# A Fourier mixer and GeGLU kernel: a sixth sequence unit as seven block products, and five gate/up units in place of three made in the first quarter

## The chip, the cores and the metric

The kernel runs on one core of one Trainium2 chip. The metric is the device time of one execution in microseconds (us). Three timed runs of the kernel before gave 705.33, 707.02 and 707.19 us; their median is 707.02 us. "The trace" is one execution that was recorded by the hardware profiler.

## What is computed

The input x is 2048 x 448. Two sublayers follow each other, each behind a layer norm and with a residual:

```python
def _A_ref(x, dft_seq_re, dft_seq_im, dft_hid_re, dft_hid_im):
    a = jnp.einsum("bsd,ed->bse", x, dft_hid_re)
    b = jnp.einsum("bsd,ed->bse", x, dft_hid_im)
    y = jnp.einsum("ts,bse->bte", dft_seq_re, a) - jnp.einsum("ts,bse->bte", dft_seq_im, b)
    return y
def _B_ref(x, w_gate, w_up, w_down):
    g = jnp.einsum("bsd,df->bsf", x, w_gate)
    u = jnp.einsum("bsd,df->bsf", x, w_up)
    return jnp.einsum("bsf,fd->bsd", _gelu(g) * u, w_down)
h = x + _A_ref(_layernorm(x, axis=-1), ...)
h2 = h + _B_ref(_layernorm(h, axis=-1), ...)
```

The gate and up weights are 448 x 1792 each, the down weight is 1792 x 448. All inputs are 32-bit floats.

## The kernel before

**Numbers.** TensorE works on 16-bit halves. Each operand is split into a high part (ScalarE, `hi_part`, L106: a scaled copy to 16 bits) and a low part (VectorE, `lo_part`, L110 and L112: what the high part left over). A product then takes three matmuls: high by high, low by high, high by low.

**Stage one, the two transforms** (up to 348 us of the trace). Sixteen row tiles of x are normalised, split and turned (x_stats L354, x_lo, x_turn), and each gives two banks of features, a and b (`feature_mm`, L457, 22 matmuls of 448 columns). Two neighbouring tiles are a "unit" u of the sequence transform; there are 8 units and 8 passes p over the output rows. `seq_mm` (L574) multiplies the weights of one pass and unit (`wr`, 128 x 1024, loaded one by one) with the features of the unit's two tiles. A plain unit does it directly: 24 matmuls of 448 columns. A unit in `S_UNITS` does it as a 2 x 2 block product with seven products in place of eight: 42 matmuls of 224 columns. For that VectorE builds sums of weight blocks (`seq_sums`, L518 to L522) and splits them too (`wss`; L106 and L112), and once for each tile sums of features (`feature_sums`, L494 to L498, and `sums_low`, L110). Units 3 to 7 are done so, units 0 to 2 are plain. Of the raw weight blocks an S unit needs three; before, these lie in places 0, 2 and 3 of `wr`, so that each split is two instructions, of 256 and of 512 columns.

**Gate/up units.** The 14 column blocks f of gate and up are combined into seven-product form too (class `Weights`: sums L643 to L649, four splits). Eleven are made during stage one and stored to DRAM piece by piece (`w_dram`); they come back by a load of 896 KB (`gw_load`, L1073). Three, `LATE = {4: 0, 8: 7, 12: 15}`, are made in the first quarter of stage two: the number is the beat (half step) at which they begin. A late unit stays in its SBUF tile for the first quarter and is stored whole to DRAM (L698) for the other three.

**Stage two, the GeGLU** goes over four quarters q of the rows, with 14 steps each (t = 14 q + f). A step is a gate/up unit (class `GateUp`, 39 matmuls of 256 columns, L1199, in three PSUM banks X, Y, Z). From the second quarter on it holds a chunk of the down product of the quarter before as well (`dn_mm`, L1144, 21 matmuls of 224 columns). In a step VectorE reads Z and writes half of `hh` (L1209), reads Y and writes the other half (L1266), and reads Z again into `c12` (L1209, shown as `c`). TensorE closes Z (`z_close`) only after the first of these. `hh` of an odd quarter lives in the pool `odd_q`, which is opened on the place of the pool `scr` as the first quarter ends (`quarter0.close()`). `scr` holds, in the first quarter, raw gate/up weights and the weight tiles of units with f % 5 of 3 and 4.

**The down weight** comes in seven chunks n (`down_load`, L230, 448 KB each), of which GpSimd makes sums (`down_sums`, L235 to L238), ScalarE and VectorE splits (`down_hi`, `down_lo`). Before, chunks 0 and 1 are loaded ahead of the first quarter into two buffers, the tags `xn` and `tt` in turn, and the splits go on during steps 1 to 15.

**What sets the order.** Each engine and the load queue run their instructions strictly as written. In stage one a planner at build time (`arranged`) places tasks by costs and due times, which a table `SHIFT` moves by kind of task. In stage two the order is written by hand: the loop over t, `late_prep` for the late units, `down_prep` for the down weight, and the table `side` of extra work by step and place in the step. All DMAs are issued by SyncE (SP), also in order, so that one that waits holds all behind it. Their ends are counted on eight lanes (DMAHW0 to DMAHW7), given out in turn.

## Time and profile before

| | |
|---|---|
| timed runs, median of three | 707.02 us |
| the profiled execution, first to last instruction | 703.5 us |
| busy: TensorE, VectorE, ScalarE, GpSimd | 697.0, 563.2, 408.0, 198.8 us |
| granted TensorE clock | 0.999 |
| stage one / first quarter / the rest, about | 348 / 61 / 294 us |

The profile names for every recorded instruction its line in the kernel, its start and its length, what it waited for, and for a DMA the time from its issue to its landing. The 703.5 us are the time from the first to the last instruction of the profiled execution, and no other time of that execution is given; the timed runs are 3.5 us longer at the median. Steps are named by t, and "the first quarter" is t = 0 to 13.

### The profile page before, as it was taken

The page shows a single profiled execution, that of the slowest core. Times are in us where ns is not written, and L with a number is a line of the kernel's source. Part 1 is how long each engine was busy: PE and PEld are TensorE (multiplying, and loading weights), DVE is VectorE, ACT ScalarE, POOL GpSimd, SP SyncE. Part 2 cuts the span into 40 slices and gives each one's busy share as a digit, 9 for nine tenths or more (in the row PEclk, how much of TensorE's full clock was granted, in tenths as well). Part 3 has the DMA queues.
Part 4 walks back from the last instruction along what each step waited for, and adds up shares of the span by engine and source line. Part 5 has one row for each costly group of instructions (what it writes and reads, how often), then busy time and mean ns, then how long its engine had stood idle before and what let it go on. Part 6 is the DMA issues. An engine that isn't in the chain of part 4 may idle for free.

```text
span 703.5 us, 15378 instructions
## 1 busy us (share of the span) xinstructions
PE 697.0 (99%) x6046; PEld 584.1 (83%) x6046; DVE 563.2 (80%) x1170; ACT 408.0 (58%) x862; POOL 198.8 (28%) x225
## 2 busy tenths in 40 slices
PE   8999999999999999999999999999999999999998
PEld 5556578878787878778888889999999999999998
DVE  6999999999999897989578877575765755786786
ACT  5776674667576565656267765555555544455432
POOL 0000000000000000001136754474664745647342
PEclk9999999999999999999999999999999999999999
DMA  9554555687988867777579665658466594545401
GB/s 330 160 128 114 142 170 184 233 245 227 228 275 202 283 177 261 262 253 281 182 258 353 204 211 170 191 180 199 170 195 190 178 200 173 181 158 166 151 27 54
DMA packets 81849, 139.74 MB, mean 199 GB/s; under 512 B 41712, under 2 KB 59376, under 8 KB 81776
## 3 DMA queue, kind: packets, MB, share of 16 engines
q1 hardware_dynamic: 81776, 138.76, 63.5%
q8 instruction: 47, 0.77, 0.5%
q14 instruction: 26, 0.21, 0.1%
HBM read 109.25 MB, written 20.19 MB: 184 GB/s over the span
## 4 chain that ended last, share of the span: by engine, by line
PE 95%; DMA 1%; ACT 1%; DVE 1%; issue 1%; SPq 0%; ACTq 0%; DVEq 0%
PE acc L574 38%; PE acc_d L1144 15%; PE pY L1199 14%; PE pZ L1199 9%; PE pX L1199 9%; PE ab L457 9%; DMA x<-in_x_dram 1%; DVE dn_w L110 0%; ACT dn_w L106 0%; SPq L429 0%; ACT xn_h L254 0%; DVE st_x L354 0%; DVE hh L1209 0%; ACT wd L106 0%; ACT g L1252 0%
## 5 line engine op out<-in xcount | busy, mean ns | idle before, releaser
L1199 PEld LDWEIGHTS <-gw 128*128 128x128 f16 x2184 | 213.1, 98 | 23.7 <-issue 1.0
L574 PE MATMUL acc<-b,ws 128*128 128x224 f16 (+1 forms) x1296 | 204.6, 301 | 0.0
L574 PEld LDWEIGHTS <-ws 128*128 128x128 f16 x1296 | 125.6, 98 | 53.2
L1199 PE MATMUL pY<-hops,gw 128*128 128x256 f16 x952 | 129.1, 273 | 0.0
L1144 PE MATMUL acc_d<-wd,dn_w 128*128 128x224 f16 x1050 | 122.3, 259 | 0.0
L574 PE MATMUL acc<-b,wss 128*128 128x224 f16 x960 | 118.2, 259 | 0.0
L235 POOL TENSOR_TENSOR wd_s<-wd 128x448 f32<-128x448 f32 x7 | 10.1, 1442 | 346.8 <-DMA wr<-in_w_seq_dram 330.0
L1144 PEld LDWEIGHTS <-dn_w 128*128 128x128 f16 x1050 | 101.1, 98 | 2.9
L574 PEld LDWEIGHTS <-wss 128*128 128x128 f16 x960 | 92.3, 98 | 0.1
L106 ACT ACTIVATE ws<-wr 128x256 f16<-128x256 f32 (+2 forms) x104 | 62.4, 637 | 41.1 <-PE acc L574 16.1
L1199 PE MATMUL pZ<-hops,gw 128*128 128x256 f16 x616 | 85.5, 273 | 0.4 <-DVE hh L1209 0.3
L1276 POOL TENSOR_TENSOR hh<-hh,c 128x256 f32<-128x256 f32 x56 | 46.3, 828 | 139.7 <-ACT c L1274 139.5
L1199 PE MATMUL pX<-hops,gw 128*128 128x256 f16 x616 | 83.3, 273 | 0.0
L112 DVE SCALAR_TENSOR_TENSOR ws<-wr,ws 128x256 f16<-128x256 f32 (+2 forms) x104 | 70.6, 709 | 1.4 <-ACT ws L106 1.3
L110 DVE TENSOR_TENSOR dn_w<-hh,dn_w 128x256 f16<-128x256 f32 x50 | 25.3, 506 | 53.1 <-ACT dn_w L106 52.8
L106 ACT ACTIVATE wss<-wsum 128x1024 f16<-128x1024 f32 x40 | 42.1, 1053 | 36.8 <-DVE wsum L522 21.1
L457 PEld LDWEIGHTS <-xT 128*128 128x128 f16 x352 | 33.9, 98 | 32.8 <-ACT xT L420 1.5
L110 DVE TENSOR_TENSOR dn_w<-dn_s,dn_w 128x640 f16<-128x640 f32 x50 | 54.6, 1092 | 7.4 <-ACT dn_w L106 6.7
L1243 ACT ACTIVATE u<-pY 128x256 f32<-128x256 f32 x56 | 21.4, 382 | 61.4 <-PE pY L1199 61.3
L1291 POOL TENSOR_TENSOR dn_s<-hh 128x256 f32<-128x256 f32 x42 | 52.8, 1258 | 0.0
L112 DVE SCALAR_TENSOR_TENSOR wss<-wsum,wss 128x1024 f16<-128x1024 f32 x40 | 48.8, 1220 | 4.1 <-ACT wss L106 4.0
L1238 ACT ACTIVATE pY<-pX 128x256 f32<-128x256 f32 x56 | 20.6, 368 | 50.3 <-PE pX L1199 50.3
(120 smaller groups left out, 936.9 us busy)
## 6 DMA issues: line engine op xcount, KB each, us to landing
gw<-w_dram SPq DMA_DIRECT2D x53, 896.0 KB, 4.8
wr<-in_w_seq_dram SPq DMA_DIRECT2D x64, 512.0 KB, 4.4
gu_raw<-in_w_gu_dram SPq DMA_DIRECT2D x28, 384.0 KB, 4.8
w_dram<-gu_p SPq DMA_DIRECT2D x33, 256.0 KB, 3.1
hx<-in_x_dram SPq DMA_DIRECT2D x8, 448.0 KB, 4.5
h_dram<-hx SPq DMA_DIRECT2D x8, 448.0 KB, 4.8
hr<-h_dram SPq DMA_DIRECT2D x8, 448.0 KB, 5.3
x<-in_x_dram SPq DMA_DIRECT2D x7, 448.0 KB, 6.9
```

Source lines behind the costliest of these rows:

```text
L106: A.activation(dst, src, AF.Copy, scale=scale)
L110: V.tensor_sub(dst, src, hi)
L112: V.scalar_tensor_tensor(dst, src, scale, hi, op0=ALU.mult, op1=ALU.subtract)
L235: G.tensor_sub(s[:, 2:4], t[:, 0:2], t[:, 2:4])
L457: PE.matmul(feat[i][r][:, :D], xT[i][:, kx, :], w[:, kw, r * D : (r + 1) * D], start=n == 0, stop=n == 10,)
L574: PE.matmul(banks[k][:, cols], lhs, rhs, start=k not in begun, stop=stop, skip_group_check=True)
L1144: PE.matmul(acc[k // 2][:, k % 2 * HD : (k % 2 + 1) * HD], a_of(la, a), b_of(lb, b), start=first and m == 0 and k % 2 == 0, stop=last and ...
L1199: PE.matmul(ps, w[:, wl, wa + ws, :], ops[:, m + ms, :], start=first and n == 0, stop=last and n == len(terms) - 1, skip_group_check=True,)
L1238: A.activation(self.Y, self.X, AF.Copy)
L1243: A.activation(self.u2, self.Y, AF.Copy, scale=SC)
L1276: G.tensor_mul(c22, c22, self.c12)
L1291: E.tensor_sub(s[:, 2:4], t[:, 1:4:2], t[:, 0:4:2])
```

## The change

Unit 2 joins the S units, so that six of eight units are seven block products. The blocks of the sequence weights are renamed (`PRODUCTS`, `seq_sums`), so that the three raw blocks of an S unit lie side by side and one instruction of 768 columns splits them. The statistics of two of the eight pairs of x tiles (units 7 and 4) are taken by ScalarE, and parts of the reciprocal root move there (`half_of`, a Square). Gate/up units in the first quarter are now five, `LATE = {4: 0, 6: 5, 9: 10, 11: 15, 13: 19}`, each in five beats in place of six, so that nine are left to stage one. The split of the normalised h of pass 3 moves from stage one to steps 0 to 4 (`ffn_sums(1, 1, ...)` and what follows); that of quarter 2 begins at step 19 in place of 14. The down weight has one buffer, the tag `v` in stage two's pool, in place of two; its first chunk is loaded in step 4, its splits run from step 6 to step 19, and chunk n + 1 is loaded when the low part of chunk n is done. The planner has other costs and another `SHIFT`.

```diff
-    S_UNITS, WR_BUFS, WS_BUFS, WSS_BUFS, STAGE_BUFS = (3, 4, 5, 6, 7), 3, 3, 2, 2
+    S_UNITS, WR_BUFS, WS_BUFS, WSS_BUFS, STAGE_BUFS = (2, 3, 4, 5, 6, 7), 3, 3, 2, 2
+    BY_SCALAR = (7, 4)
...
+    def half_of(mv, tag, pool=small, of=1):
+        n = mv.shape[1]
+        r = pool.tile([P, 4, n], F32, tag=f"r{n}" if pool is small else f"r_{tag}", name=f"r_{tag}")
+        A.activation(r[:, 1], mv[:, :, 1], AF.Identity, scale=-0.5 / (of * X_SC**2), bias=half_eps)
+        return r
...
-        V.tensor_mul(r[:, 2], r[:, 0], r[:, 0])
+        if by_vector:
+            V.tensor_mul(r[:, 2], r[:, 0], r[:, 0])
+        else:
+            A.activation(r[:, 2], r[:, 0], AF.Square)
...
     def down_load(n):
-        wd32[n] = fops.tile([P, 4, HD], F32, tag="tt" if n % 2 else "xn", name=f"wd32_{n}")
+        wd32[n] = fpool.tile([P, 4, HD], F32, tag="v", name=f"wd32_{n}")
...
+    def x_moments(i, tiles):
+        if i == tiles[0]:
+            norm_x[tiles] = small.tile([P, 2, 2], F32, tag="mv2", name=f"mv_x{i}")
+        act_moments(norm_x[tiles][:, tiles.index(i), :], xt[i][0], junk)
...
-        V.tensor_add(s[:, 0:2], r[:, 1:2].to_broadcast([P, 2, 2 * P]), r[:, 0:4:3])
+        V.tensor_add(s[:, 0:2], r[:, 0:1].to_broadcast([P, 2, 2 * P]), r[:, 1:3])
...
-            return [(w[0], slice(0, 1), r[:, 0:1]), (w[0], slice(1, 3), r[:, 2:4])]
+            return [(w[0], slice(0, 3), r[:, 1:4])]
...
-    SHIFT = {"copy": -31.8, "fhigh": -68.2, "fhighp": -18.1, "flow": 9.9, "fsum": 12.9, "guhi": 1.2, "gulo":
+    SHIFT = {"copy": 481.5, "fhigh": -975.2, "fhighp": -890.3, "flow0": -229.1, "flow1": -167.7,
...
+    IN_FFN = 3
...
+            if p == IN_FFN:
+                continue
...
-    LATE = {4: 0, 8: 7, 12: 15}
+    LATE = {4: 0, 6: 5, 9: 10, 11: 15, 13: 19}
...
-    t = fixed(len(slots) - 14, 9, "SP", 0.1, lambda: down_load(0), last_e, lag=6.0, kind="dload")
-    fixed(len(slots) - 8, 9, "G", 4.0, lambda: down_sums(0), [t], kind="dsum")
...
-    down_load(1)
...
         n, odd = divmod(t, 2)
         if odd:
-            if n < NC:
+            if 0 <= n < NC:
                 down_lo(n, 1)
-                if n + 2 < NC:
-                    down_load(n + 2)
-            if n + 1 < NC:
+            if n + 1 < NC and n >= 0:
                 down_sums(n + 1)
-        elif n < NC:
+        elif 0 <= n < NC:
             down_hi(n, 0)
             down_lo(n, 0)
+            if n + 1 < NC:
+                down_load(n + 1)
+    WD0 = 6
+    def down_mid(t):
+        n, odd = divmod(t - WD0, 2)
+        if odd and 0 <= n < NC:
+            down_hi(n, 1)
...
+        (0, 1, lambda: ffn_sums(1, 1, (0,))),
...
+        (4, 4, lambda: down_load(0)),
+        (5, 4, lambda: down_sums(0)),
...
+        t0 = NF + 5 + 4 * j
+            (0 if j else -5, 1, lambda j=j: ffn_norm_act(2, j, hp[2, j])),
...
+    for f, n in LATE.items():
+        for k in range(5):
+            at(late_beats, n + k, (f, k))
...
-            if t > 0:
-                down_prep(t - 1)
+            do(t, 2)
+            down_prep(t - WD0)
             late_prep(2 * t + 1)
+            do(t, 4)
```

On SyncE, at the end of the first quarter, the DMAs stand as follows before (`gw` loads a unit's weights, `w_dram<-gw` stores a late unit, `wd32` loads a chunk of the down weight, `hr` loads rows of h; the brackets name the counters waited for):

```order
L1073 DMA gw13_5190<-w_dram13_164 128x3584 [waits DMAHW3_49,DMAHW1_49,PE_49]
L1073 DMA gw14_5253<-w_dram0_151 128x3584 [waits DMAHW6_49,DMAHW4_49,PE_49]
L230 DMA wd32_6_5317<-in_w_down_dram 128x896 [waits DMAHW5_49,DMAHW7_49,DVE_49,Pool_49]
L1073 DMA gw15_5384<-w_dram1_152 128x3584 [waits DMAHW0_49,PE_49]
L698 DMA w_dram12_163<-gw12_5149 128x3584 [waits DVE_49,Activation_49]
L1073 DMA gw16_5453<-w_dram2_153 128x3584 [waits DMAHW7_49,PE_49]
L1073 DMA gw17_5606<-w_dram3_154 128x3584 [waits DMAHW4_49,PE_49]
```

The same place on SyncE now (`gu_raw` loads the raw weights of a gate/up unit):

```order
L247 DMA wd32_2_5257<-in_w_down_dram 128x896 [waits DMAHW2_49,DMAHW4_49,DVE_49,Pool_49]
L673 DMA gu_raw13_5262<-in_w_gu_dram 128x768 [waits DMAHW7_49,DMAHW0_49,DVE_49]
L673 DMA gu_raw13_5262<-in_w_gu_dram 128x768 [waits DMAHW6_49]
L734 DMA w_dram9_162<-gw9_5051 128x3584
L1121 DMA gw14_5333<-w_dram0_153 128x3584 [waits PE_49]
L247 DMA wd32_3_5401<-in_w_down_dram 128x896 [waits DMAHW1_49,DMAHW4_49,DVE_49,Pool_49]
L734 DMA w_dram11_164<-gw11_5224 128x3584
L1121 DMA gw15_5475<-w_dram1_154 128x3584 [waits DMAHW3_49,DMAHW2_49,PE_49]
L247 DMA wd32_4_5539<-in_w_down_dram 128x896 [waits DMAHW1_49,DVE_49,Pool_49]
L1121 DMA gw16_5541<-w_dram2_155 128x3584 [waits DMAHW5_49,PE_49]
L734 DMA w_dram13_166<-gw13_5364 128x3584 [waits DMAHW6_49]
```

One store stood here and now there are three, for units 9, 11 and 13; the loads of the down weight, of which the last stood here, are now only at chunks 2 to 4, and the loads of units 14 to 16 stand between them.

On VectorE, as step 13 passes into step 14, the rows are before (`dn_w` is a split for the down product, `wd` one of the down weight; the last row is the first write into the second quarter's `hh`):

```order
L1209 SCALAR_TENSOR_TENSOR c12_12_5441<-pZ_12_5350,u2_12_5363 128x256 [waits PE_49,Pool_49]
L110 TENSOR_TENSOR dn_w0_5443<-hh0_4599,dn_w0_5443 128x256 [waits Activation_49]
L110 TENSOR_TENSOR dn_w0_5443<-dn_s0_5312,dn_w0_5443 128x640 [waits DVE_49,Activation_49]
L112 SCALAR_TENSOR_TENSOR wd_4572<-wd_s_5_5319,wd_4572 128x1120
L1209 SCALAR_TENSOR_TENSOR hh0_4599<-pZ_13_5415,u3_13_5479 128x256 [waits Activation_49]
L1266 SCALAR_TENSOR_TENSOR hh0_4599<-pY_13_5400,g1_13_5460 128x256 [waits PE_49]
L1209 SCALAR_TENSOR_TENSOR c12_13_5508<-pZ_13_5415,u2_13_5428 128x256 [waits PE_49,Pool_49]
L112 SCALAR_TENSOR_TENSOR wd_4572<-wd32_6_5317,wd_4572 128x448 [waits DMAHW5_49,Activation_49]
L110 TENSOR_TENSOR dn_w1_5527<-hh0_4599,dn_w1_5527 128x256 [waits Activation_49]
L110 TENSOR_TENSOR dn_w1_5527<-dn_s1_5378,dn_w1_5527 128x640 [waits DVE_49,Activation_49]
L1209 SCALAR_TENSOR_TENSOR hh1_5516<-pZ_14_5482,u3_14_5550 128x256 [waits DMAHW3_49,DMAHW1_49,Activation_49]
```

The same place on VectorE now:

```order
L1264 SCALAR_TENSOR_TENSOR c12_12_5530<-pZ_12_5437,u2_12_5450 128x256 [waits PE_49,Pool_49]
L112 TENSOR_TENSOR dn_w0_5532<-hh0_4652,dn_w0_5532 128x256 [waits Activation_49]
L112 TENSOR_TENSOR dn_w0_5532<-dn_s0_5395,dn_w0_5532 128x640 [waits DVE_49,Activation_49]
L114 SCALAR_TENSOR_TENSOR wd_4625<-wd32_3_5401,wd_4625 128x448 [waits DMAHW1_49,Activation_49]
L1264 SCALAR_TENSOR_TENSOR hh0_4652<-pZ_13_5504,u3_13_5567 128x256 [waits Activation_49]
L1321 SCALAR_TENSOR_TENSOR hh0_4652<-pY_13_5491,g1_13_5548 128x256 [waits PE_49]
L1264 SCALAR_TENSOR_TENSOR c12_13_5598<-pZ_13_5504,u2_13_5517 128x256 [waits PE_49,Pool_49]
L114 SCALAR_TENSOR_TENSOR wd_4625<-wd_s_3_5470,wd_4625 128x1120 [waits Activation_49]
L112 TENSOR_TENSOR dn_w1_5620<-hh0_4652,dn_w1_5620 128x256 [waits Activation_49]
L112 TENSOR_TENSOR dn_w1_5620<-dn_s1_5465,dn_w1_5620 128x640 [waits DVE_49,Activation_49]
L1264 SCALAR_TENSOR_TENSOR hh1_5609<-pZ_14_5572,u3_14_5643 128x256 [waits DMAHW6_49,DMAHW7_49,DVE_49,Activation_49]
```

The splits between are of chunk 3 in place of chunks 5 and 6, and the first write into `hh1` now waits on DMA lanes 6 and 7. Lane 6's last user ahead of it is the store of unit 13, whose tile (13 % 5 is 3) lies in `scr`; lane 7's is the store of unit 9.

More of the change, by code (lines that the diff above doesn't have):

```diff
@@ L92 @@
     G.memset(eps_t, EPS / X_SC**2)
+    half_eps = const.tile([P, 1], F32, name="half_eps")
+    G.memset(half_eps, -0.5 * EPS / X_SC**2)
     warm = const.tile([P, 1], F32, name="warm")
@@ L328 @@
     xt, xs, xT, norm_x = {}, {}, {}, {}
+    by_scalar = tuple((2 * u, 2 * u + 1) for u in BY_SCALAR)
+    junk = p1.tile([P, D], F16, name="junk")
     x_pairs = x.rearrange("(u g p) d -> u p g d", g=2, p=P)
@@ L501, in sums_high @@
     def sums_high(i):
-        t = bop[i] = dft.tile([P, 2, 7, HD], F16, name=f"b{i}")
+        if i == tiles_of[-1][1]:
+            t = p1.tile([P, 2, 7, HD], F16, tag="xs", name=f"b{i}")
+        else:
+            t = dft.tile([P, 2, 7, HD], F16, name=f"b{i}")
+        bop[i] = t
         hi_part(t[:, 0], b32[i][:, 1:8])
@@ L714 @@
     mixed = plain[:]
-    for n, s in zip((1, 3, 4, 5, 7), S_UNITS):
+    for n, s in zip((1, 2, 3, 5, 6, 7), S_UNITS):
         mixed.insert(n, s)
@@ L763, in chain @@
         for k, cost in enumerate(costs):
-            last = [add(engine, cost, due, lambda k=k: step(k == 0), after=last, kind=kind)]
+            on, cost = cost if isinstance(cost, tuple) else (engine, cost)
+            last = [add(on, cost, due, lambda k=k: step(k == 0), after=last, kind=kind)]
         return last[0]
@@ L834 @@
         room = [steps[where["U", *units[g - WS_BUFS]]]] if g >= WS_BUFS else []
-        size = 0.9 if is_s(u) else 1.0
-        high = add("A", size, T[n] - 1.6 if g else -20.0, lambda p=p, u=u: seq_high(p, u), begin=-4.0, after=[load] + room, kind="whigh" if g else None)
-        low = add("V", 1.02 if is_s(u) else 1.16, T[n] - 0.4 if g else -20.0, lambda p=p, u=u: seq_low(p, u), after=[high], kind="wlow" if g else None)
+        size = 0.82 if is_s(u) else 1.0
+        high = add("A", size, T[n] - 1.6 if g else -20.0, lambda p=p, u=u: seq_high(p, u), begin=-4.0, after=[load] + room, kind="whigh" if g else "whigh0")
+        low = add("V", 0.87 if is_s(u) else 1.16, T[n] - 0.4 if g else -20.0, lambda p=p, u=u: seq_low(p, u), after=[high], kind="wlow" if g else "wlow0")
         done_with[g] = [low]
@@ L867 @@
         m = [add("A", 1.75, t0 + 9.0 + 4 * g, lambda q=q, j=j, g=g, p=p: ffn_moments(q, j, hp[q, j], g, junk_of(e_of[p])), after=[mixed_in], kind="mom") for g in range(2)]
-        t = add("A", 0.25, t0 + 14.0, lambda q=q, j=j: ffn_root(q, j), after=m, kind="hroot")
-        t = chain("V", (0.2, 0.1, 0.1, 0.1), t0 + 15.0, lambda q=q, j=j: ffn_rstd_steps(q, j), [t], kind="hrstd")
+        t = add("A", 0.45, t0 + 14.0, lambda q=q, j=j: ffn_root(q, j), after=m, kind="hroot")
+        t = chain("V", RSTD, t0 + 15.0, lambda q=q, j=j: ffn_rstd_steps(q, j), [t], kind="hrstd")
         last_e, h_done[p] = m, [store, t]
@@ L1051 @@
             seq_mm(p, u, u == mine[0], u == mine[-1])
-        if t == p1_end:
-            first.close()
+    first.close()
     right.close()
@@ L1325, in dn_drain @@
     def dn_drain(p):
-        v = [ftile(f"v{k}", 1, f"v{k}_{p}", D) for k in range(2)]
+        v = fpool.tile([P, 2, D], F32, tag="v", name=f"v_{p}")
+        v = [v[:, k] for k in range(2)]
         return Drain(hr[p], acc_d[p], v, 1.0 / (H_SC * W_SC))
@@ L1416 @@
     odd_q = None
-    late_beats = {n + k: (f, k) for f, n in LATE.items() for k in range(6)}
-    assert len(late_beats) == 6 * len(LATE)
+    late_beats = {}
+    for f, n in LATE.items():
+        for k in range(5):
+            at(late_beats, n + k, (f, k))
     def late_prep(beat):
-        if beat not in late_beats:
-            return
-        f, k = late_beats[beat]
-        gu[f].beat(k)
-        after = [v for v in LATE if v > f]
-        if k == 3 and after:
-            gu_late(after[0])
-        if k == 5:
-            gw[f] = gu[f].w
+        for f, k in late_beats.pop(beat, ()):
+            gu[f].beat(k)
+            after = [v for v in LATE if v > f]
+            if k == 2 and after:
+                gu_late(after[0])
+            if k == 4:
+                gw[f] = gu[f].w
     cur = GateUp(0)
@@ L1451 @@
         d = t - NF
-        if d >= 0 and d % NC == 1:
+        if d >= 0 and d % NC == (4 if d // NC == 1 else 1):
             hr_load(d // NC)
@@ L1465 @@
                 gu[t].store()
-            if t > 0 and t % 2 == 0 and t < 2 * NC:
-                down_hi(t // 2 - 1, 1)
+            do(t, 1)
+            down_mid(t)
             nxt.z_open()
@@ L1556 @@
     part_store(7, 1, 1)
-    assert not side
+    assert not side and not late_beats
 def _tiles(inputs):
```

135 lines of the change are left out of this document (94 added, 41 removed).

## The prediction

> **What bounds the kernel now.** I read the page first, for the chain that ended last. Its summary by engine:
>
> ```profile
> PE 95%; DMA 1%; ACT 1%; DVE 1%; issue 1%; SPq 0%; ACTq 0%; DVEq 0%
> ```
>
> Nearly all of that chain is matmuls, so a change gains what it takes off TensorE (PE) and loses every stretch in which PE has to wait. Next I read the same chain in order of time (start, length, line, matmuls). `acc` rows are the sequence transform: x24 is one plain unit, x42 one unit of seven products. `pX` and `pY` rows are steps of the first quarter.
>
> ```profile
> 61.82 4.03 PE acc L574 x42
> 65.85 8.32 PE ab L457 x44
> 74.17 4.54 PE acc L574 x24
> ...
> 99.38 248.30 PE acc L574 x2100
> ...
> 400.92 1.20 PE pX L1199 x11
> 403.43 1.20 PE pY L1199 x11
> 405.18 1.20 PE pX L1199 x11
> ```
>
> The 2100 matmuls are 21 plain and 38 seven-product units: 21 x 4.54 + 38 x 4.03 = 248.5 us, against 248.30. From 99 to 348 us PE waits for nothing. Two `pX` rows are 405.18 - 400.92 = 4.26 us apart, which is a whole step: the first quarter is packed too. Last, the busy time of the engines by stage (columns: PE, PEld, VectorE = DVE, ScalarE = ACT, GpSimd = POOL):
>
> ```profile
> 27.80:99.40 71.60, 71.60 (x422) 40.95 (x421) 66.85 (x155) 49.48 (x80) 0.00 (x0) 1.00 0.55 144
> 99.40:347.70 248.30, 248.30 (x2102) 202.11 (x2101) 224.76 (x445) 153.52 (x291) 4.77 (x3) 1.00 0.76 237
> 347.70:409.30 61.60, 61.58 (x565) 54.95 (x564) 48.34 (x87) 42.62 (x100) 31.84 (x33) 1.00 0.74 258
> ```
>
> VectorE is the next in line: 291.6 of 319.9 us (91%) in stage one, 48.3 of 61.6 (78%) in the first quarter.
>
> **The sixth seven-product unit: PE gains.** In each of 8 passes 4.54 us become 4.03: 8 x 0.51 = 4.1 us off the path. All of it counts, since these rows have no wait between them. The price of 42 short matmuls depends on whether weight loads keep up:
>
> ```profile
> L574 PEld LDWEIGHTS <-ws 128*128 128x128 f16 x1296 | 125.6, 98 | 53.2
> ```
>
> A load is 98 ns here, and 42 pairs take 4.03 us, 96 ns a pair: loads just keep up. The Trainium skill (TensorE: Matmul & The Clock Gate, LDWEIGHTS (loading the stationary operand)) puts a load at its columns over 1.2, so 107 ns for 128; my estimate from that page is 42 x 107 = 4.48 us a unit and a gain of only 0.5 us. The measured row decides against it.
>
> **The same unit on VectorE.** The costliest rows by shape (count, busy, mean ns):
>
> ```profile
> L112 DVE SCALAR_TENSOR_TENSOR wss<-wsum,wss 128x1024 f16<-128x1024 f32 x40 | 48.8, 1220 | 4.1 <-ACT wss L106 4.0
> L112 DVE SCALAR_TENSOR_TENSOR ws<-wr,ws 128x1024 f16<-128x1024 f32 x24 | 29.7, 1238 | 1.0 <-ACT ws L106 0.9
> L518 DVE TENSOR_TENSOR wsum<-wr 128x512 f32<-128x512 f32 x40 | 28.4, 709 | 9.0 <-DMA wr<-in_w_seq_dram 8.8
> L112 DVE SCALAR_TENSOR_TENSOR ws<-wr,ws 128x512 f16<-128x512 f32 x40 | 27.3, 684 | 0.1
> ...
> L520 DVE TENSOR_TENSOR wsum<-wsum,wr 128x256 f32<-128x256 f32 x40 | 16.8, 419 | 0.3
> ```
>
> A pass gains sums (709 + 2 x 419) and their split (1220), and the raw split falls from 1238 to about 961 (768 columns, between the rows for 512 and 1024): 2.49 us, times 8 = 19.9. Raw blocks side by side save the other 40 units 684 + about 419 - 961 = 0.14 us each: 5.7. The unit's two feature tiles, by the rows of tile `b` (min/median/max ns):
>
> ```profile
> L112 DVE SCALAR_TENSOR_TENSOR b<-ab,b x12: 592/614/618, 21.9 to 55.2; 128x448 f16<-128x448 f32 x12
> L494 DVE TENSOR_TENSOR b<-b x10: 615/624/626, 38.2 to 100.2; 128x448 f32<-128x448 f32 x10
> L496 DVE TENSOR_TENSOR b<-b x10: 380/384/393, 39.4 to 100.9; 128x224 f32<-128x224 f32 x10
> L498 DVE TENSOR_TENSOR b<-b x10: 381/384/391, 40.7 to 101.3; 128x224 f32<-128x224 f32 x10
> L110 DVE TENSOR_TENSOR b<-b,b x10: 1782/1786/1793, 42.9 to 103.9; 128x1568 f16<-128x1568 f32 x10
> ```
>
> Each pays 624 + 2 x 384 + 1786 - 2 x 614 = 1.95 us: 3.9 for two. Against this two gate/up units leave, and the split of pass 3. First the busy time in stage one on `gu_s` (four sums and two of four splits, 11 units), then on `tt` (four row pairs):
>
> ```profile
> 27.00:348.00 321.00, 36.44 (x66) 13.48 (x22) 1.00 0.71 215
> ```
>
> ```profile
> 60.00:348.00 288.00, 12.23 (x36) 4.32 (x8) 1.00 0.72 223
> ```
>
> A unit is 36.44 / 11 + 0.684 + 0.419 = 4.4 us, two 8.8; the pass at least 12.23 / 4 = 3.1. Sum: 19.9 - 5.7 + 3.9 - 8.8 - 3.1 = +6.2 us, and x statistics and root steps that go to ScalarE take more off, which I leave unpriced. VectorE then has at most 297.8 of 315.8 us, 94%. It fits, with 18 us spare where there were 28. The cost lies between nothing and the whole 4.1 (if VectorE paced the stage); I take 0.5, near the lower end, since the 248.30 row shows no wait at 91%. ScalarE, at 203.0 of 319.9, has room for what it gets.
>
> **The first late unit.** Its raw weights are now loaded behind four stores of unit 12, whose last splits stand behind the last sequence split. Here are the loads (KB each, median us to landing), and that of the down weight:
>
> ```profile
> gw<-w_dram SPq DMA_DIRECT2D x53, 896.0 KB, 4.8
> wr<-in_w_seq_dram SPq DMA_DIRECT2D x64, 512.0 KB, 4.4
> gu_raw<-in_w_gu_dram SPq DMA_DIRECT2D x28, 384.0 KB, 4.8
> ...
> wd<-in_w_down_dram SPq DMA_DIRECT2D x7, 448.0 KB, 5.9
> ```
>
> If nothing hides it VectorE waits 4.8 us in step 0 ahead of what PE needs; if the stores are early it waits for nothing. I take 0.5.
>
> **The first quarter on VectorE.** It gets two late units (8.8) and the split of pass 3 (3.1 or more), and three of seven chunks of the down weight leave. At some 57 of 61.6 us (93%) it still fits, but runs late by up to a us, and its order is fixed.
>
> **The end of the first quarter: where I expect the loss.** The store of unit 13 must land before VectorE may write into the second quarter's `hh`, because the unit's tile lies where `hh1` goes. Stores of a late unit, us from issue to landing (min/median/max of three):
>
> ```profile
> DMA to landing us min/median/max: 8.0/8.6/9.2
> ```
>
> One of them in the load queue's timeline, and the `gw` load that waited for it, 8.67 us later:
>
> ```profile
> 401.36 0.38 SPq L698 DMA_DIRECT2D w_dram<-gw  x1
> 410.03 4.43 SPq L1073 DMA_DIRECT2D gw<-w_dram  x2
> ```
>
> The write into `hh1` and the matmuls that wait for it (they add to Z, which it reads), before:
>
> ```profile
> 412.84 0.41 DVE L1209 SCALAR_TENSOR_TENSOR hh<-pZ,u 128x256 f32<-128x256 f32 x1
> ```
>
> ```profile
> 413.40 0.71 PE L1199 MATMUL pZ<-hops,gw 128*128 128x256 f16 x5
> ```
>
> The earliest case: ahead of that store stand the loads of chunk 4 and unit 16. The first waits for the low part of chunk 3, which now stands where VectorE had this row:
>
> ```profile
> 406.69 1.32 DVE L112 SCALAR_TENSOR_TENSOR wd<-wd_s,wd 128x1120 f16<-128x1120 f32 x1
> ```
>
> It ends at about 407.3 (0.61 for 448 columns, as in tile `b`); with three issues of 0.3 the store goes at 408.2 and lands at 416.2 at the earliest. PE then goes on at 416.6 in place of 413.4: 3.2 us lost.
>
> The later case is a chain. With one buffer, chunk n + 1 is loaded only when GpSimd has summed chunk n. The sums of six chunks on GpSimd (third column; 18.96 / 6 = 3.2 us each):
>
> ```profile
> 348.30:411.00 62.70, 7.89 (x6) 6.77 (x6) 18.96 (x18) 1.00 0.73 254
> ```
>
> A round is 5.9 + 3.2 = 9.1 us, where two steps are 8.5. Chunk 0 is asked for behind the transposes that follow step 4, at about 372.5: step 5 starts at 405.18 - 8 x 4.26 = 371.1. It lands at 378.4, and after two more rounds and the sums of chunk 2, 399.8, the load of chunk 3 may go; VectorE's part of chunk 2, late in a full quarter, makes it 400.5. Behind it stands the store of unit 11 (landed 409.4), behind that, waiting for it, the load of unit 15, then chunk 4, unit 16 and the store of unit 13, at 410.4, landed 419.0. PE goes on at 419.4: 6.0 us lost. Nothing hides this, since PE is packed up to there and cannot pass `z_close`. Unit 15 itself lands at about 414.5, inside the same wait. The raw weights of unit 13, queued behind chunk 2 until 390.7, land at about 396, a us or two late in step 10; that wait is part of the 6.0, since the chain does not run by PE. I take 6.0, the later case, since every one of its links is written in the order; with loads at 7.0 and stores at 9.2 it would be 9.
>
> **The sum.** 703.5 - 4.1 + 0.5 + 0.5 + 6.0 = 706.4 us of span. The timed median is 3.5 above the span (707.02 against 703.5), so 709.9 us. A measurement of this kernel can tell about 0.3%, 2.1 us, from no change.
>
> **Rivals.** (1) The store is in time, and the change is faster. Price: 6.0 less, 703.9 us. It decides at a landing by 412.9, which needs a store of under 4.7 us at the earliest case. Against it speak all three stores (8.0 at least); for it, that a load of the same 896 KB takes 4.8 and that those stores ran beside other traffic. Chance 0.12. The Trainium skill (DMA: Bandwidth & Descriptors, Anatomy of one DMA) fits 2.0 us plus bytes over 436 GB/s for its path, an estimate of 4.1 us for this store, and warns that completion can be surprisingly late where HBM is written; by the formula the store would be in time, and the three measured stores contradict it. (2) The short chain: chunks land early, and only the earliest case holds. 3.2 in place of 6.0: 707.1 us, no change that can be told. Chance 0.22. (3) VectorE, at 94% in stage one, paces PE there as well: some 3 us more, 712.9. For it speaks that its order is strict; against it, that the unpriced x statistics leave it. Chance 0.10. (4) Weight loads set the pace and the PE gain is 0.5: 713.5. The 4.03 us row says no; 0.01. The forecast keeps 0.55, its own range 708.5 to 713.
>
> Faster takes rival 1 and a little: 0.13. Same takes rival 2 and the low edge of the forecast: 0.27. Slower is 0.60. The range, 704.2 to 714, leaves out half of rival 1 and the high end of the chain.
>
> **What would show it.** The plain units of pass 1 on: x42 in six of eight, and stage one ending some 4 us sooner. A wait of VectorE for a `w_dram` store at the first write into `hh`, with PE idle or stretched by 3 to 9 us around step 14. GpSimd waiting for `wd` loads in each odd step. I am wrong if the store of unit 13 lands before step 14 reaches `z_close`, or if stage one ends less than 3 us sooner.

## The result, and the profile after

The changed kernel takes 731.62 us (median of four runs, 730.01 to 734.46) against 706.35 us for the kernel before beside it: a ratio of 1.0366, with a 95% interval of 1.0339 to 1.0393. It is 25 us slower; the forecast was 3 us slower, with a range that ended at 714. The traced execution took 734.46 us, with a span of 732.7, so 1.8 us lie outside the span. (The forecast's 3.5 us were these 1.8 and the fact that the traced execution of before was, by these 1.8 us, the fastest of its three.) Of the executions reported below, two were disturbed, one of k1a and the traced one of k2b; they took some 1883 us and are left out of the medians.

The chain that ended last, by engine, was nearly all PE before. Now a quarter of it is something else:

```profile
PE 74%; DVE 10%; DMA 9%; ACT 3%; issue 2%; SPq 1%; POOL 1%; DVEq 0%; ACTq 0%
```

Where that quarter lies is shown by the busy time of the engines by stage, in the columns that the prediction showed. The stretches are stage one, the first quarter with the two steps behind it, the rest of the second quarter, and what is left:

```profile
27.50:343.70 316.20, 315.96 (x2663) 256.25 (x2662) 297.02 (x537) 212.35 (x365) 0.00 (x0) 1.00 0.64 196
343.70:440.00 96.30, 75.53 (x631) 64.23 (x629) 59.00 (x119) 49.10 (x118) 32.80 (x35) 0.90 0.68 220
440.00:520.00 80.00, 76.70 (x717) 69.86 (x716) 55.66 (x109) 43.79 (x104) 46.33 (x50) 0.99 0.58 182
520.00:732.70 212.70, 209.43 (x2024) 195.88 (x2022) 146.47 (x310) 100.45 (x253) 115.66 (x132) 1.00 0.49 156
```

Stage one is as forecast: PE waits 0.24 us in it, VectorE has 297.0 of 316.2 us (94%). All the loss is behind it. From 343.7 to 440 PE is idle for 20.8 us, and the granted clock (the column after POOL) is 0.90 where it was 1.00.

PE's timeline gives the stops, each with what ended it in brackets (start, length, matmuls):

```profile
342.33 0.64 PE L610 MATMUL acc<-b,ws 128*128 128x224 f16 x5
...
344.24 0.82 PE L1254 MATMUL pX<-hops,gw 128*128 128x256 f16 x6
...
354.00 0.81 PE L1254 MATMUL pZ<-hops,gw 128*128 128x256 f16 x6 [1.33 <-DVE c L1264]
...
371.68 1.36 PE L1254 MATMUL pY<-hops,gw 128*128 128x256 f16 x11
...
383.30 2.51 PE L1254 MATMUL pY<-hops,gw 128*128 128x256 f16 x11 [7.20 <-ACT pY L1293]
...
409.13 1.23 PE L1254 MATMUL pZ<-hops,gw 128*128 128x256 f16 x5 [4.37 <-DVE hh L1264]
...
436.28 1.22 PE L1254 MATMUL pZ<-hops,gw 128*128 128x256 f16 x5 [6.57 <-DVE hh L1264]
```

There are four stops over 1 us up to step 14, of 1.3, 7.2, 4.4 and 6.6 us; the shorter ones bring the sum to 24.0 us. Behind a long stop the same eleven matmuls take 2.51 us where they took 1.36 ahead of it. The engine named in the brackets was itself held by a DMA each time. For the stop of 1.3 us VectorE had waited 2.44 us for the raw weights of unit 4. For the three long ones it was first ScalarE, whose in-order queue stands at the high part of unit 9; then VectorE at the raw weights of unit 13, and at its first write into `hh1`:

```profile
381.77 0.94 ACT L108 ACTIVATE gw<-gu_raw 128x512 f16<-128x512 f32 x2 [8.85 <-DMA w_dram<-gw]
```

```profile
407.09 0.79 DVE L679 TENSOR_TENSOR gu_s<-gu_raw 128x384 f32<-128x384 f32 x1 [3.67 <-DMA gu_raw<-in_w_gu_dram]
...
435.80 0.42 DVE L1264 SCALAR_TENSOR_TENSOR hh<-pZ,u 128x256 f32<-128x256 f32 x1 [7.18 <-DMA w_dram<-gw]
```

Only the last of these is the wait that the prediction built on. The first is one that it did not see: units 4 and 9 both have f % 5 = 4, so unit 9 is made in the tile of unit 4, and its first write waits until unit 4 has been stored. That store stands in the load queue (start, time of issue) between two pairs of transposes, which are new there, since the split of pass 3 was moved into the first quarter:

```profile
369.07 3.72 SPq L332 DMA_TRANSPOSE hops<-xs  x2
372.89 0.54 SPq L1121 DMA_DIRECT2D gw<-w_dram  x1
373.47 0.43 SPq L734 DMA_DIRECT2D w_dram<-gw  x1
373.94 4.94 SPq L332 DMA_TRANSPOSE hops<-xs  x2
378.93 0.58 SPq L247 DMA_DIRECT2D wd<-in_w_down_dram  x1
```

The store was issued at 373.47 and landed at 381.75, though unit 4's last split had ended at 360.

PE's 24 us of stops do not make up the whole. PE is busy for 701.4 us where 697.0 - 4.1 = 692.9 were due, 8.5 us more. By the starts of the matmuls behind the three long stops, 6.8 of these are matmuls at a lower clock (1.8, 2.5 and 2.6 us). The rest is something else: k1b, below, is busy for 694.9 us at a clock of 1.00, also 2 us above what was due, and where those come from stays open. Together: 703.5 - 4.1 + 24 + 8.5 = 731.9, against a span of 732.7.

### The profile page after: what moved, and what is told of

It reads as the page before. It is cut to its first block, busy times and chain, and to the rows that moved or that the text cites. A ratio compares the mean times of both kernels' runs of the same rounds, so it can differ in the third digit from the quotient of the medians.

```text
span 732.7 us, 15592 instructions
## 1 busy us (share of the span) xinstructions
PE 701.4 (96%) x6190; PEld 600.4 (82%) x6190; DVE 579.7 (79%) x1140; ACT 422.8 (58%) x870; POOL 196.4 (27%) x226
## 4 chain that ended last, share of the span: by engine, by line
PE 74%; DVE 10%; DMA 9%; ACT 3%; issue 2%; SPq 1%; POOL 1%; DVEq 0%; ACTq 0%
PE acc L610 25%; PE acc_d L1191 14%; PE pY L1254 12%; PE pZ L1254 8%; PE pX L1254 8%; PE ab L489 7%; DMA wr<-in_w_seq_dram 3%; DMA w_dram<-gw 3%; DMA gu_raw<-in_w_gu_dram 2%; DVE ws L114 1%; DVE dn_w L112 1%; DVE wsum L554 1%; DVE wss L114 1%; DVE wd L114 1%; DMA w_dram<-gu_p 1%
## 5 line engine op out<-in xcount | busy, mean ns | idle before, releaser
L1254 PEld LDWEIGHTS <-gw 128*128 128x128 f16 x2184 | 216.3, 99 | 50.7 <-issue 24.9
L610 PE MATMUL acc<-b,ws 128*128 128x224 f16 (+1 forms) x1248 | 187.2, 288 | 0.2 <-DVE ws L114 0.2
L610 PEld LDWEIGHTS <-ws 128*128 128x128 f16 x1248 | 120.7, 98 | 36.1 <-DVE ws L114 0.7
L610 PE MATMUL acc<-b,wss 128*128 128x224 f16 x1152 | 141.7, 259 | 0.0
L610 PEld LDWEIGHTS <-wss 128*128 128x128 f16 x1152 | 110.8, 98 | 0.0
L108 ACT ACTIVATE wss<-wsum 128x1024 f16<-128x1024 f32 x48 | 50.6, 1054 | 47.3 <-DVE wsum L558 34.0
L108 ACT ACTIVATE ws<-wr 128x768 f16<-128x768 f32 (+1 forms) x64 | 56.8, 890 | 29.0 <-PE acc L610 16.6
L114 DVE SCALAR_TENSOR_TENSOR ws<-wr,ws 128x768 f16<-128x768 f32 (+1 forms) x64 | 65.0, 1018 | 0.5 <-ACT ws L108 0.5
L114 DVE SCALAR_TENSOR_TENSOR wss<-wsum,wss 128x1024 f16<-128x1024 f32 x48 | 58.6, 1220 | 3.1 <-ACT wss L108 2.7
L1293 ACT ACTIVATE pY<-pX 128x256 f32<-128x256 f32 x56 | 20.7, 369 | 48.4 <-PE pX L1254 48.3
L489 PE MATMUL ab<-wh_hi,xT 128*128 128x448 f16 x224 | 45.6, 352 | 1.2 <-DVE b L114 0.4
```

The lines of the kernel that those rows point to most:

```text
L108: A.activation(dst, src, AF.Copy, scale=scale)
L114: V.scalar_tensor_tensor(dst, src, scale, hi, op0=ALU.mult, op1=ALU.subtract)
L489: PE.matmul(feat[i][r][:, :D], xT[i][:, kx, :], w[:, kw, r * D : (r + 1) * D], start=n == 0, stop=n == 10,)
L610: PE.matmul(banks[k][:, cols], lhs, rhs, start=k not in begun, stop=stop, skip_group_check=True)
L1254: PE.matmul(ps, w[:, wl, wa + ws, :], ops[:, m + ms, :], start=first and n == 0, stop=last and n == len(terms) - 1, skip_group_check=True,)
L1293: A.activation(self.Y, self.X, AF.Copy)
```

## The experiments

**The single stops.** Each of four runs takes one cause away from the changed kernel. The first moves the store of unit 4:

```diff
             if k == 4:
                 gw[f] = gu[f].w
+                if f in (4,):
+                    gu[f].store()
...
-            if t in LATE:
+            if t in LATE and t not in (4,):
                 gu[t].store()
```

> The changed kernel, with the store of unit 4 issued right after its last split (step 2) in place of step 4. In its trace PE stops 7.2 us in step 6 while ScalarE waits for that store (issued 373.5, landed 381.8), and runs at half speed for some 4 us behind it (about 2.0 us more). Theory A, single waits: each stop of PE has one transfer as its cause, and its price is the stop and the slow stretch behind it, so the time falls by 9.2 to about 722.4. Theory B, the next in line: the load of chunk 0 of the down weight landed at 384.8, 3 us after the store, and ScalarE needs it one step later; then most of the stop stays under another name, and the time falls by 0 to 3, to 728.5 to 731.6.

Measured: 729.31 us, ratio to before 1.0326 (1.0302 to 1.0350), 2.3 us less than the changed kernel. The wait for the store is gone, and ScalarE stands a few microseconds later at the next late transfer, chunk 0 of the down weight:

```profile
381.42 0.58 ACT L108 ACTIVATE wd<-wd 128x448 f16<-128x448 f32 x1 [4.34 <-DMA wd<-in_w_down_dram]
```

PE stops for 0.7, 2.0 and 0.8 us there, 3.5 in place of 7.2, and no slow matmuls follow. By the median theory B holds: the store alone was not the price. The traced execution, at 726.80 us, was the fastest of the four, so B is right in kind, but half of the stop stays and not most of it. The next kernel loads chunk 0 ahead of the transposes as well:

```diff
-        (4, 4, lambda: down_load(0)),
+        (1, 1, lambda: down_load(0)),
```

> As e1, and the load of chunk 0 of the down weight is issued in step 1, ahead of the transposes, in place of behind them in step 4. Theory A: the same as e1, 722.4, since the load was not the cause. Theory B: only now does the stop of step 6 go, about 722.4 here and 728.5 or more in e1. Theory C, VectorE is the limit of the first quarter (it has no idle time from 387.3 to 403.4 in the changed kernel): the stop goes here, but the one near step 10 grows by some 4 us, and the time is about 726.

Measured: 725.59 us, 1.0284 (1.0267 to 1.0301), 6.0 less than the changed kernel. The stop of 7.2 us is gone but for 1.2 us. The time is the one that theory C gave, but not for its reason: the stop of step 10 became 3.9 us, no longer than before. What is left of the 9.2 us of theory A are small stops (1.9, 0.6, 1.2 and 1.1 us).

The third kernel stores unit 13, and only it, right after its last split (the edit of e1 with 13 for 4).

> The changed kernel, with the store of unit 13 issued right after its last split (step 11) in place of step 13, ahead of the loads of chunk 4 and units 15 and 16. The split ended at 419.2, the stop of 6.6 us began at 429.7, and stores took 8 to 10 us. Theory A: the store lands at 427.7 to 429.5, the stop goes with its slow stretch (2.7), and the time falls by 8 to 9.3, to about 723. Theory B: PE stops there for something else that comes as late (the load of unit 15, the splits of chunk 3), and the time falls by under 3.

Measured: 724.12 us, 1.0257 (1.0234 to 1.0280), 7.5 less. PE no longer stops for over 0.5 us around step 14. Theory A holds, though its 8 to 9.3 us were a little too much; the wait on which the forecast rested is real and is worth what it said, and a little more. The fourth gives the raw weights of unit 13 a buffer of their own:

```diff
-            self.raw = pool.tile([P, 2, 6, P], F32, tag="raw", name=f"gu_raw{f}")
+            self.raw = pool.tile([P, 2, 6, P], F32, tag="raw2" if f == 13 else "raw", name=f"gu_raw{f}")
...
-            if k == 2 and after:
+            if k == (0 if f == 11 else 2) and after:
                 gu_late(after[0])
```

> The changed kernel, with a buffer of its own for the raw weights of unit 13, which are loaded in step 7 in place of step 8 and need not wait until VectorE has split those of unit 11. Theory A: the stop of 4.4 us near step 10 and its slow stretch (2.7) go, 724.6; the stop at step 14 stays as it is, 6 to 7 us, since its store waits behind work of step 13 that moves along with PE. Theory D, the chain of the down weight's chunks does not run by PE (the later case of the forecast): what is gained at step 10 is lost at step 14, whose stop grows to 11 to 13 us, and the time stays within 2 us of 731.6.

Measured: 728.15 us, 1.0316 (1.0301 to 1.0332), 3.5 less, half of what theory A gave. The stop of 4.4 us became two of 1.7 and 1.3. At step 14, which PE now reached 4 us sooner, the stop is as long as ever:

```profile
432.09 1.23 PE L1254 MATMUL pZ<-hops,gw 128*128 128x256 f16 x5 [6.24 <-DVE hh L1264]
```

It was 6.6 us in e1 and 6.5 in e2 too. Theory D, which is the chain of the forecast, would have made it longer each time. It falls: the store of unit 13 waits behind the load of chunk 4, which waits for VectorE's low part of chunk 3 in step 13, and that moves along with PE.

**All of them.** The three edits together, with all late units stored right after their last split:

> The edits of e2, e3 and e4 together: every late unit is stored right after its last split, chunk 0 of the down weight is loaded in step 1, and the raw weights of unit 13 have a buffer of their own. They gave 6.0, 7.5 and 3.5 us apart. Theory A, single waits: they add up, 731.6 - 17.0 = 714.6, with no stop of PE over 2 us and its clock near 1.00 throughout. Theory C, VectorE (or the chain of chunks) is the limit of the first quarter: taking one stop away moves PE on to the next, and the three together give under 12 us, 719.6 or more.

Measured: 717.89 us, 1.0164 (1.0121 to 1.0207), 13.7 less of 17.0. The largest stop is 2.9 us and the clock is back at 1.00, but the fourteen stops of stage two still add up to 13.8 us, and the kernel is 11.6 us above before. The interval, 714.8 to 720.9 us, reaches from theory A's time to theory C's and does not decide; the trace does, since small stops have come where the long ones went, as theory C says.

**What a stop costs.** In the kernel before, copies that nothing reads hold ScalarE in step 6:

```diff
+    block = const.tile([P, 512], F32, name="block")
+    G.memset(block, 0.0)
...
+            for _ in range(15 if t == 6 else 0):
+                A.activation(block, block, AF.Copy)
             late_prep(2 * t)
```

> The kernel before, with fifteen copies of 512 columns on ScalarE (some 0.6 us each, 9 us in all) put ahead of its work in step 6, which nothing reads. ScalarE has some 1.5 us to spare in a step, so PE should stop once, for 7 to 8 us. Face value: the time rises by the stop alone, 7 to 8 us. The stretch theory: the granted clock falls behind a stop of this length, matmuls take twice their time for some 4 us, and the time rises by 2 to 2.7 us more than the stop, some 10 us.

Measured: 716.25 us, 1.0142 (1.0123 to 1.0161), so 10.0 us more (8.7 to 11.4) for one stop of 8.0 us: the stretch theory. The same edit with 7 in place of 15:

> As c15_stop_long, with seven copies in place of fifteen, some 3.9 us on ScalarE. Fifteen stopped PE for 8.0 us and cost 9.9. PE should stop for some 3.5 us here. Face value: 709.8. The stretch theory: stops of up to 2.0 us had no slow matmuls behind them in the traces so far, those of 3.9 and more had 1 to 2.7 us; a stop of 3.5 us costs another 1 to 2 us, 711 to 712.

Measured: 710.09 us, 1.0057 (1.0037 to 1.0076), so 4.3 us more (2.6 to 5.4) for a stop of 2.7 us: face value, by the time and by the clock behind it. The windows ahead of, in and behind the stop show the difference; first fifteen copies, then seven (the clock is the column after POOL):

```profile
370.00:381.00 11.00, 11.00 (x103) 9.85 (x101) 10.15 (x18) 9.31 (x20) 6.64 (x6) 1.00 0.85 306
381.00:389.70 8.70, 0.70 (x7) 0.48 (x6) 0.36 (x1) 8.35 (x15) 0.00 (x0) 0.76 0.91 359
389.70:397.00 7.30, 7.30 (x56) 6.04 (x56) 4.07 (x9) 3.96 (x12) 4.26 (x5) 0.82 0.11 24
397.00:405.00 8.00, 8.00 (x75) 7.17 (x74) 7.44 (x12) 6.41 (x16) 4.75 (x5) 1.00 0.44 156
```

```profile
370.00:382.00 12.00, 12.00 (x113) 10.73 (x111) 11.19 (x20) 10.29 (x23) 7.58 (x7) 1.00 0.80 292
382.00:386.00 4.00, 1.29 (x13) 1.01 (x11) 0.91 (x2) 3.90 (x9) 0.00 (x0) 1.00 1.04 413
386.00:393.00 7.00, 7.00 (x67) 6.29 (x65) 5.53 (x11) 4.96 (x12) 4.72 (x5) 1.00 0.92 316
```

Behind the stop of 8.0 us PE gets through 56 matmuls in 7.3 us, where full speed gives 67 in 7.0, the number behind the stop of 2.7 us. So the long stop pays again, some 1.3 us here by the starts of its matmuls, and the short one does not. A stop of 0.7 and 0.9 us in stage one that came with the edit in both runs makes up part of the rest; its cause stays open.

**Fewer late units.** f4 is the changed kernel with stores right after the last split, chunk 0 in step 1, and four late units; f3 has the three of before:

```diff
-    LATE = {4: 0, 6: 5, 9: 10, 11: 15, 13: 19}
+    LATE = {4: 0, 6: 5, 9: 10, 11: 15}
```

> The changed kernel with every late unit stored right after its last split and chunk 0 loaded in step 1, and with four late units in place of five: unit 13 is made in stage one again. With it go its store, its raw load and 4.4 us of VectorE from the first quarter, and VectorE in stage one rises from 297 to some 301 of 316 us (95%). Theory A: the stops at steps 10 and 14 go, and the one of step 6; left are some 1.5 us at step 0 and 3 us of small stops from step 15 on, so 706.4 - 3.7 + 5 = about 708. Theory E, VectorE is the limit of stage one too: stage one, 316.4 us in the changed kernel, grows by 2 us or more, and the time is 710 or more.

Measured: 721.34 us, 1.0216 (1.0195 to 1.0237).

> As f4, with the three late units of the kernel before (4, 8 and 12, in five beats each, at its own beats), so that eleven units are made in stage one beside the sixth seven-product unit. VectorE in stage one has some 306 of 316 us (97%). Theory A: no stop of the first quarter over 2 us is left, about 707. Theory E: stage one grows by 4 us or more against the changed kernel's 316.4, which takes the whole gain of the sixth unit, and the time is 710 or more.

Measured: 727.88 us, 1.0310 (1.0289 to 1.0331). Both times are in the range of theory E, but neither theory had the place right. The waits of PE, f4 first and then f3 (total, times, longest):

```profile
PE acc L610 <- ACT acc L595: 5.8, 1, 5.8
PE pY L1254 <- ACT u L1298: 3.1, 1, 3.1
```

```profile
PE pY L1254 <- ACT pY L1293: 9.7, 2, 9.1
PE pZ L1254 <- DVE c L1264: 5.0, 1, 5.0
```

In f4 the order of stage one no longer fits its work: a copy on ScalarE comes 5.8 us late at 245 us. In f3 PE keeps its pace through stage one, but its last two gate/up units are finished only behind it, and PE stands for 9.1 and then, at the raw weights of unit 4, for 5.0 us. The order had been set for nine units. So h1 and h3 repeat four and three late units with the planner's `SHIFT` set anew for each, unit 4's raw weights loaded ahead of units 2 and 3, and the chunks one step earlier:

```diff
-    gw_load(2)
-    gw_load(3)
+    gu_late(min(LATE))
+    gw_load(2)
+    gw_load(3)
...
-    gu_late(min(LATE))
...
-    WD0 = 6
+    WD0 = 5
...
-        s = wd_s[n] = fops.tile([P, 5, HD], F32, tag="xs", name=f"wd_s_{n}")
+        s = wd_s[n] = (scr if n < 2 else fops).tile([P, 5, HD], F32, tag="wds" if n < 2 else "xs", name=f"wd_s_{n}")
```

> The kernel of f4 (four late units) with three things changed: the planner's due times are set anew for ten units in stage one (f4 had kept those for nine, and PE stopped 5.8 us at 245 for a late copy on ScalarE); the raw weights of unit 4 are loaded ahead of units 2 and 3; and the sums of the first two chunks have a place of their own, so that the chunks begin a step earlier (step 5). Theory A: stage one takes 316 to 317 us, no stop over 2 us is left, and of small ones 3 to 4 us: 706.4 - 3.7 + 4 = about 707. Theory E, VectorE is the limit of stage one: it takes 319 us or more, 710 or more.

Measured: 712.23 us, 1.0086 (1.0063 to 1.0109). From the first sequence unit on, stage one now runs without a stop, with VectorE at 300.3 of 317.4 us, and step 0 too, so the load of unit 4's raw weights was what had stopped it. But PE still stops once for 3.5 us, where unit 11's raw weights landed 9 us after their issue behind two transposes, a chunk and unit 10. The time is one that theory E allows, but stage one stays below its 319 us, so VectorE was not the limit there.

> As h1, with the three late units of the kernel before and due times set for eleven units in stage one (in f3 the last two of them ran on into the first quarter, where PE stopped 9.1 and 5.0 us). VectorE in stage one has 97%. Theory A: 706.4 - 3.7 + 1 for stage one + 2 of small stops = about 706. Theory E: stage one takes 319 us or more, or its last unit again ends behind it and PE stops for over 2 us in steps 0 to 2; 709 or more.

Measured: 711.33 us, 1.0077 (1.0062 to 1.0092). Stage one's stops add up to some 2 us with VectorE at 301.8 of 316.5 us; the largest later one is 1.8 us. Three of the stops, 1.8 us at 245 to 260, are waits for VectorE's splits of sequence weights, so with VectorE at 95% stage one gives back half of the gain: more than theory A, less than theory E. Whether the amount of work or its order is the reason stays open.

**What is left in e5.** Here GpSimd's three sums of each chunk are left out for one memset:

```diff
-        G.tensor_sub(s[:, 2:4], t[:, 0:2], t[:, 2:4])
-        t22 = t.rearrange("p (a b) d -> p a b d", a=2)
-        G.tensor_add(s[:, 0:2], t22[:, :, 0], t22[:, :, 1])
-        G.tensor_add(s[:, 4], t[:, 0], t[:, 3])
+        G.memset(s, 0.0)
```

> The kernel of e5, with GpSimd's three sums of each chunk of the down weight (3.2 us a chunk) left out: one memset of the tile stands for them, so that the down product is not the reference's. In e5 VectorE has no idle time from 390.9 to 411, and its instructions that read SBUF take up to three times as long while GpSimd works (a split of two pieces 2.42 us in place of 1.02, a sum 1.35 in place of 0.42). Theory F, VectorE is slowed by GpSimd: they take their shorter times, the three small stops of PE at 396 to 408 (3.9 us) go, and the time is about 714, 4 us below e5's 717.9. Theory C, VectorE has too much to do there in any case: the stops stay, and the time is within 1.5 us of 717.9.

Measured: 711.78 us, 1.0079 (1.0058 to 1.0101), 6.1 less than e5 (6.4 by the spans of the two traces). VectorE's groups from 390 to 411 us (mean ns behind the comma), e5 and then this kernel:

```profile
L114 DVE SCALAR_TENSOR_TENSOR gw<-gu_raw,gw 128x512 f16<-128x512 f32 x2 | 2.8, 1414 | 0.0
...
L114 DVE SCALAR_TENSOR_TENSOR wd<-wd,wd 128x448 f16<-128x448 f32 x2 | 2.0, 1022 | 0.0
...
L1264 DVE SCALAR_TENSOR_TENSOR hh<-pZ,u 128x256 f32<-128x256 f32 x4 | 1.6, 412 | 0.0
```

```profile
L1261 DVE SCALAR_TENSOR_TENSOR hh<-pZ,u 128x256 f32<-128x256 f32 x5 | 2.1, 415 | 0.1
...
L114 DVE SCALAR_TENSOR_TENSOR gw<-gu_raw,gw 128x512 f16<-128x512 f32 x2 | 1.4, 680 | 0.0
...
L114 DVE SCALAR_TENSOR_TENSOR wd<-wd,wd 128x448 f16<-128x448 f32 x2 | 1.2, 612 | 0.0
```

The same split of 512 columns falls from 1414 to 680 ns, that of 448 from 1022 to 612; an instruction that reads PSUM stays at 412 to 415. These two rows fell the most. Others fell less (splits of 512 columns of the sums from 810 to 743, splits of 256 from 908 to 681) and one sum not at all (596 and 629), since GpSimd still has 9.28 us of other work in these 21 us, where it had 14.76. Theory F holds in kind: with GpSimd at work VectorE's SBUF work takes up to twice its time in the rows shown. The stops behind 396 us fell from 3.9 to 0.8. The 6.1 us are not all of this kind, since the memset also ends sooner than the sums and lets the next chunk be loaded, and no run tells the two apart; one stop of 1.9 us at 389 is new.

The last three put the split and the four transposes of pass 3 back into stage one, with `SHIFT` set anew:

```diff
-    IN_FFN = 3
+    IN_FFN = None
...
-        (0, 1, lambda: ffn_sums(1, 1, (0,))),
...
-        (4, 4, lambda: ffn_transpose(1, 1, (3,))),
```

> The kernel of e5 (five late units) with the split and the transposes of pass 3 back in stage one, as in the kernel before, and the planner's due times set anew for it. In e5 the load queue spends 8.6 us on four transposes in steps 4 and 5, the sums of chunk 0 wait for them until 385.0, and PE stops for 1.1 us at 380 and 2.9 us at 386. Theory T, the moved transposes hold the queue: both stops go, 717.9 - 4 = 714; the small ones behind them (3.9 us) stay. Theory C, VectorE and the chain of chunks in the first quarter are the cause: the stops only move, and the time is within 1.5 us of 717.9.

Measured: 712.51 us, 1.0086 (1.0069 to 1.0103), 5.4 less than e5. No stop is left between 354 and 391 us. Theory T holds: the transposes had held the load queue, and with it chunk 0 and unit 10. The stops at 396 to 402 stay (1.7 and 1.3 us).

> As k1a, with the raw weights of unit 4 loaded ahead of units 2 and 3 and the chunks of the down weight begun three steps earlier (step 3 in place of 6), so that GpSimd's sums lie less on the steps of units 9 to 13 and the last chunk is split in step 16 in place of 19. Theory A, single waits: no stop over 1 us is left, of small ones 2 to 3 us, and the sixth unit's 3.7 us show for the first time: 706.4 - 3.7 + 3.5 = about 706. Theory C: the stops move to other steps, and the time is 709 or more.

Measured: 710.50 us, 1.0069 (1.0052 to 1.0085). Its waits of PE, and the first rows of its second stage:

```profile
PE pZ L1246 <- DVE hh L1256: 6.6, 9, 1.8
```

```profile
343.57 0.82 PE L1246 MATMUL pX<-hops,gw 128*128 128x256 f16 x6
```

Stage two begins at 343.57 in place of 347.52 before: the sixth unit's 4 us are there in full. Most of what gives them back is nine waits for VectorE's writes into `hh`, 6.6 us, 4.1 of them at 388 to 406 us, where units 9 to 13 and GpSimd's sums meet on VectorE as in e5 (a split of 512 columns of the sums takes 1.25 us there). So theory C is right about the rest. No stop of over 0.3 us is left in stage two ahead of 388 us.

> As k1b with four late units (unit 13 made in stage one), due times set anew. VectorE in stage one has some 304 of 316.5 us (96%). Theory A: stage one takes 317 us, no stop over 1 us in the first quarter: 704 to 705. Theory E, VectorE is the limit of stage one: it takes 319 us or more and the time is 707 or more.

Measured: 710.28 us, 1.0051 (1.0031 to 1.0071). The time is one of theory E's, but its trace cannot be read, so whether VectorE paced stage one there stays open. None of the thirteen kernels built on the change beats the kernel before.

## Why the prediction was wrong, point by point

The step that failed is the first quarter. The prediction said that it "still fits, but runs late by up to a us", and put one wait of PE behind stage one into its sum, 6.0 us at step 14. The trace has two more long stops of PE ahead of that one, 7.2 us for the store of unit 4 and 4.4 us for the raw weights of unit 13, 6.8 us of slowed matmuls behind these two and that of step 14, and some 4.5 us of small stops.

**The gain on PE: right.** 8 x 0.51 = 4.1 us were forecast. Stage two begins 3.3 us sooner in the changed kernel, whose first sequence unit started 0.4 us later and which has the 0.24 us of stops, so 4.0; and 4.0 us sooner in k1b.

**VectorE in stage one: right.** 94% forecast, 94% measured, with 0.24 us of stops for the 0.5. Rival 3 falls, and so does rival 4.

**The first late unit: right in kind.** 0.5 us forecast, within 0 to 4.8; measured 1.3, and h1 and k1b took it away by loading the raw weights first.

**"It still fits, but runs late by up to a us": this step failed.** The sum of VectorE's work was not too small. It should have come out lower: three chunks of the down weight take 3 x 13.38 / 6 = 6.7 us of VectorE in the trace before (tile `wd`, first row), so 48.3 + 8.8 + 3.1 - 6.7 = 53.5 us were due in place of 57. 53.98 were measured in steps 0 to 13 of the changed kernel (second row, third busy time):

```profile
347.50:408.50 61.00, 13.38 (x12) 1.00 0.74 259
```

```profile
344.20:424.40 80.20, 66.31 (x562) 56.76 (x560) 53.98 (x108) 44.38 (x108) 27.41 (x29) 0.91 0.72 233
```

What failed is to read a wait from a sum over a whole quarter. In the long stops PE waited for transfers, not for the amount of VectorE's work. And with the transfers moved the work still lies unevenly: in e5 (first row) and in k1b (second) VectorE has hardly any idle time over some 20 us, where the late units' work falls on the same steps as GpSimd's sums:

```profile
390.00:411.00 21.00, 16.94 (x150) 14.42 (x149) 20.38 (x33) 13.16 (x31) 14.76 (x14) 1.00 0.72 268
```

```profile
388.00:406.00 18.00, 14.03 (x125) 11.96 (x123) 17.93 (x26) 11.15 (x26) 13.93 (x14) 1.00 0.51 184
```

That is the rest that no moved transfer removed here. That GpSimd's sums lengthen the work there is shown by g1 on e5; how much of k1b's rest they make is not, since no run leaves them out of k1b. The trace before had the sign of it: the work on `gu_s` takes 12.05 / 3 = 4.0 us of VectorE for a late unit in the first quarter, and the price taken was 36.44 / 11 = 3.3 from stage one, where GpSimd is all but idle.

**The waits that the step did not have.** The edit of `LATE` was costed by its instructions and by which tile gives its place to `hh1`, but not by which late units share a tile. Unit 9 in unit 4's tile gave the largest stop, 7.2 us, and when that store was moved (e1) chunk 0, behind the transposes, was next. The raw weights of unit 13 were named, but as "a us or two" inside the 6.0; they were a stop of their own, 4.4 us, because unit 13 begins only two beats after unit 11 gives its raw buffer free. The four transposes of pass 3 were not priced at all, though they take 8.7 us of the load queue ahead of chunk 0 (k1a).

**The store of unit 13: right wait, right size, wrong chain.** 6.0 us forecast, 6.6 measured, and 7.5 won by e3. Rival 1 falls. But the forecast's reason for 6.0 in place of 3.2 was a chain of chunks that does not run by PE, and in e1, e2 and e4 the stop stayed as it was when PE came sooner. The link is the one that the prediction called the earliest case and gave to rival 2: low part of chunk 3, chunk 4, store. So rival 2 had the link, and its 3.2 us were too few: the store took 10.2 us from issue to landing, where the 8.0 of the earliest case stood, and that is 2.2 of the 3.4 us. That the 6.0 came near is luck.

**The price of a stop: this step failed as well.** Stops were taken at their length. Three of them, from 4.4 to 7.2 us, each brought slow matmuls behind it, 6.8 us in all.

So the terms of the sum were about right where they existed: -4.0, 0.2, 1.3 and 6.6 for -4.1, 0.5, 0.5 and 6.0. By the spans the forecast was 706.4 and the trace 732.7. Between them lie two stops without a term of their own (11.6 us), slow matmuls (6.8), small stops of the first two quarters (some 4.5), and some 2 us of PE's busy time whose cause stays open. The range was too narrow because it held the size of one wait only, when the same edit had put two more stores, two more sets of raw weights and four transposes on one in-order queue.

## What to carry to other kernels

When work is moved into a stage that has no slack, list for every buffer in it who had it last and which transfer frees it, and every transfer that stands ahead of that one in its queue; a new wait is rarely alone, and behind the first one that is removed stands the next. Price a PE stop of more than some 3 us at its length and, going by these traces, 1.3 to 2.6 us more. Sum a VectorE budget step by step, not over a stage, and with the durations that its instructions have while GpSimd runs, if GpSimd will run.
